# A fused transformer block on one core: V and the softmax weights on head-major partitions, all softmax results through DRAM, and a new order

## The chip, the cores and the metric

The kernel runs on one core of one Trainium2 chip. The metric is the device time of one execution in microseconds, as a median over runs: 238.28 us (three runs, 237.95 to 239.0). A core has five engines with queues of their own: TensorE (PE: matmuls, with weight loads as PEld), VectorE (DVE), ScalarE (ACT), GpSimd (POOL) and SyncE (SP), which here only issues transfers. Each engine executes its instructions strictly in the order in which the program gives them, and waits on semaphores for the others.

## The reference

The program is one block with adaptive layer norm, on x of 2048 positions and 512 features. A conditioning vector gives six modulation vectors. Attention has 32 heads of 16 features and looks back over eight positions, two apart.

```python
mod = (_silu(c) @ w_mod).reshape(c.shape[0], 6, 1, -1)       # sa, ca, ga, sb, cb, gb
h = _layernorm(x) * (1 + ca) + sa
q, k, v = split(h @ wqkv)                                    # 32 heads of 16
idx = pos[:, None] - arange(8) * 2                           # window of 8, step 2; negative ones masked
attn = softmax(where(mask, (q . k[idx]) * 16 ** -0.5, -1e9))
x = x + ga * (sum_w(attn * v[idx]) @ wo)
h = _layernorm(x) * (1 + cb) + sb
x = x + gb * ((gelu(h @ w_gate) * (h @ w_up)) @ w_down)      # hidden 1792
```

Inputs and outputs are bf16.

## The kernel before

The 2048 positions are worked in four groups (`sg` 0 to 3) of 512. For each group the steps are:

- **Norm and transposition.** DVE and ACT take the statistics of x (`bn_stats`, or sums on ACT), POOL raises to the power −0.5 (`rstd`), DVE normalises (`xn`). The result is transposed to features on partitions (`hT`), on PE for group 0 and 1, by a transposing transfer for 2 and 3.
- **Projections.** Twelve sets of four 128x512 matmuls give q, k and v (`qkv_ps`), which ACT copies to SBUF as bf16 (`qT`, `kT`, `vT`). Partition p of these holds features of head p // 4.
- **Logits.** For each of four feature slices j, DVE multiplies `qT` with eight shifted views of `kT` in one instruction of 128x4096 (`pq`). PE sums over the features of a head with narrow matmuls, 32 columns wide and four side by side, against the constant `Mph`: eight for each j (`LTp`).
- **Softmax.** DVE takes the maximum over the window, subtracts, ACT applies exp, DVE sums, inverts and multiplies (`e`): partitions are head and quarter of the positions.
- **Weights times V.** The weights are needed on other partitions (`PT`: four window places times 32 heads). For group 0 sixteen narrow PE transposes (`PTp`) and two ACT copies make `PT`; groups 1 to 3 store `e` to DRAM (`escr`) and read it back in four loads. V takes a similar way: `vT` is stored in one DRAM array `vscr` for all positions, and four loads, each to 32 partitions, put the four shifted copies into `V`, in runs of 1040 bytes. POOL zeroes the start of `V` for group 0. DVE multiplies `PT` and `V` for each j (`pv`, 128x4096), PE sums over the four places and two halves with `Msum` (`o_ps`), ACT copies (`oT`).
- **Output projection, second norm, FFN.** `x_ps`, then the norm again (`h`), 14 pairs of gate and up projections (`g_ps`, `u_ps`), GELU and copy on ACT, their product on DVE (`hht`), and the down projection (`y_ps`).

The order is not found by a scheduler at run time. Every step is a generator (a "thread") that yields operations with their engine; the table `ORDER` lists which thread is advanced next, so this one list of numbers sets the order of the instructions on each engine and of the transfers in SP's queue. A transfer that waits holds up everything issued behind it. The steps that the change touches are `setup` (POOL's constants), `qkv_ev` (copies of v), `vload`, `soft` and `pt_dma` (weights), `pv` and `pv_mm`. The head of the program also has 17 matmuls on zeros (`warm_ps`) which compute nothing that is used, and the products of the modulation vectors (`modT_ps`, `gR_ps`).

Of the kernel before, what the change touches and what calls it, by code (L numbers as in the profile page):

```python
# [16 lines left out]
PT_DMA = (1, 2, 3)  # L17

ORDER = [
# [87 lines left out]
def kernel(  # L107
# [13 lines left out]
    nc = tc.nc  # L121
# [4 lines left out]
    SG = 512  # L126
    NSG = S // SG
    CPS = SG // P
    DT = D // P
    FT = F // P  # L130
    VH = 16
    VR = S + VH

    def pool(name, bufs, **kw):
        return ctx.enter_context(tc.tile_pool(name=name, bufs=bufs, **kw))

    const = pool("const", 1)
    wts = pool("wts", 1)
# [554 lines left out]
    def soft(sg):  # L693
# [38 lines left out]

        if sg in PT_DMA:
            return
# [250 lines left out]
```

## Time and profile before

| | |
|---|---|
| median of three runs | 238.28 us (237.95 to 239.0) |
| the profiled execution, from first to last instruction | 235.7 us |
| PE busy | 229.0 us, 97% |
| DVE busy | 170.0 us, 72% |
| ACT busy | 150.5 us, 64% |
| POOL busy | 23.6 us, 10% |
| granted clock of PE | 1.00 in every stretch |
| moved by transfers | 30.21 MB, 128 GB/s in the mean |

The profile gives no time of its own for the execution apart from this span; the 2.6 us to the median lie outside the first and last instruction or between executions. A row of a timeline reads: start in us, length in us, engine, line of the kernel, operation, what is written and read, shape, count; in brackets the idle time of the engine before it and what ended it. A row can hold several instructions (x4); its length runs to the end of the last, and matmuls overlap, so the starts of neighbouring rows tell more than lengths. In the list of groups the numbers behind the bar are the busy time, the mean of one in ns, and the idle time in front with its releaser. In the list of transfers they are KB each and the median us from issue to landing.

### The profile page before, as it was taken

What the parts mean: (1) busy time and instruction counts of PE and PEld (TensorE: products, weight loads), DVE (VectorE), ACT (ScalarE), POOL (GpSimd) and SP (SyncE); (2) the same over time, 40 slices, a digit from 0 to 9 for tenths busy, and PEclk for the clock granted to TensorE, in tenths of its full rate; (3) what the DMA queues carried; (4) which work ended last, traced back from release to release, by engine and by line L of the source; (5) the groups of instructions that cost most, each with busy time, mean ns of one, the idle gap of its engine ahead of it and who ended that gap; (6) DMA issues with size and microseconds to landing.
All of it is one profiled execution on the core that took longest, in us unless ns stands there. A gap on an engine that the chain in (4) does not pass through costs nothing.

```text
span 235.7 us, 3655 instructions
## 1 busy us (share of the span) xinstructions
PE 229.0 (97%) x1376; PEld 108.6 (46%) x1388; DVE 170.0 (72%) x240; ACT 150.5 (64%) x283; POOL 23.6 (10%) x43
## 2 busy tenths in 40 slices
PE   7899899999999999999999999999999999999995
PEld 2755355434644444443444444444444444444443
DVE  3898999999999999989899787259295421222222
ACT  4799978796997558943867592446737325667400
POOL 2525471000100000040000010000001000000000
PEclk9999999999999999999999999999999999999999
DMA  6997987999969929607301972520000061000011
GB/s 212 375 361 210 209 214 138 217 376 347 195 161 241 298 75 201 112 3 178 90 0 32 211 123 48 144 56 0 0 3 1 22 134 45 3 0 0 0 47 45
DMA packets 36265, 30.21 MB, mean 128 GB/s; under 512 B 14872, under 2 KB 34328, under 8 KB 36248
## 3 DMA queue, kind: packets, MB, share of 16 engines
q1 hardware_dynamic: 35968, 29.72, 49.7%
q8 instruction: 11, 0.18, 0.4%
q10 hardware_dynamic: 280, 0.26, 0.3%
q14 instruction: 6, 0.05, 0.1%
HBM read 22.37 MB, written 4.98 MB: 116 GB/s over the span
## 4 chain that ended last, share of the span: by engine, by line
PE 79%; DVE 10%; DMA 5%; POOL 3%; issue 1%; ACT 0%; DVEq 0%; POOLq 0%
PE g_ps L851 21%; PE u_ps L851 21%; PE y_ps L863 14%; PE qkv_ps L606 11%; PE x_ps L818 6%; DMA x<-in_A_x_dram 5%; DVE pq L671 4%; PE o_ps L797 3%; POOL rstd L471 3%; PE LTp L685 2%; DVE xn L448 1%; PE y_ps L875 1%; DVE pv L778 1%; DVE st L430 1%; DVE e L729 1%
## 5 line engine op out<-in xcount | busy, mean ns | idle before, releaser
L851 PE MATMUL g_ps<-h,Wg 128*128 128x512 bf16 x224 | 57.5, 379 | 0.0
L851 PE MATMUL u_ps<-h,Wu 128*128 128x512 bf16 x224 | 57.5, 379 | 0.0
L863 PE MATMUL y_ps<-Wd,hht 128*128 128x512 bf16 x203 | 45.6, 379 | 0.4
L885 ACT ACTIVATE gl<-g_ps 128x512 bf16<-128x512 f32 x56 | 33.7, 601 | 17.5 <-PE g_ps L851 15.4
L892 ACT CAST ub<-u_ps 128x512 bf16<-128x512 f32 x56 | 32.9, 587 | 16.2 <-PE u_ps L851 16.1
L606 PE MATMUL qkv_ps<-hT,wqkv 128*128 128x512 bf16 x180 | 41.0, 380 | 0.0
L903 DVE TENSOR_TENSOR hht<-gl,ub 128x512 bf16<-128x512 bf16 x56 | 23.0, 421 | 24.4 <-ACT ub L892 24.4
L778 DVE TENSOR_TENSOR pv<-PT,V 128x4096 bf16<-128x4096 bf16 x16 | 36.0, 2288 | 3.0 <-DMA PT<-escr 3.0
L671 DVE TENSOR_TENSOR pq<-qT,kT 128x4096 bf16<-128x4096 bf16 x16 | 36.4, 2296 | 0.0
L851 PEld LDWEIGHTS <-Wg 128*128 128x128 bf16 x224 | 21.7, 98 | 26.9 <-issue 1.3
L851 PEld LDWEIGHTS <-Wu 128*128 128x128 bf16 x224 | 21.7, 98 | 26.8 <-issue 0.8
L863 PEld LDWEIGHTS <-hht 128*128 128x128 bf16 x210 | 20.6, 98 | 24.7
L606 PEld LDWEIGHTS <-wqkv 128*128 128x128 bf16 x180 | 19.6, 114 | 18.6 <-issue 2.3
L471 POOL TENSOR_TENSOR rstd<-rstd,neghalf 128x4 f32<-128x4 f32 (+1 forms) x9 | 12.8, 1427 | 149.0 <-DVE rstd L460 77.6
L910 DVE TENSOR_TENSOR ot<-y_ps,x 128x512 bf16<-128x512 f32 x15 | 10.2, 690 | 20.0 <-PE y_ps L863 19.8
L532 ACT ACTIVATE h<-h,modT,scl 128x512 bf16<-128x512 bf16 x12 | 8.8, 805 | 20.3 <-DMA h<-xn 20.3
L818 PE MATMUL x_ps<-woP,oT 128*128 128x512 bf16 x60 | 15.1, 379 | 0.2
L430 DVE BATCH_NORM_STATS2 st<-x 128x6 f32<-128x512 bf16 x19 | 12.9, 677 | 3.1 <-DMA x<-in_A_x_dram 2.9
L827 DVE TENSOR_TENSOR x<-x_ps,x 128x512 bf16<-128x512 f32 x16 | 10.8, 688 | 5.4 <-PE x_ps L818 5.3
L808 ACT CAST oT<-o_ps 128x512 bf16<-128x512 f32 x16 | 8.8, 588 | 4.3 <-PE o_ps L797 4.3
L408 ACT ACTIVATE gl<-x 128x512 bf16<-128x512 bf16 x13 | 8.3, 645 | 3.2 <-DVE x L827 2.9
L685 PE MATMUL LTp<-pq,Mph 128*32 128x512 bf16 x128 | 9.1, 382 | 1.3 <-DVE pq L671 1.3
(85 smaller groups left out, 184.7 us busy)
## 6 DMA issues: line engine op xcount, KB each, us to landing
V<-vscr SPq DMA_DIRECT2D x12, 520.0 KB, 10.5
wm<-in_w_mod_dram SPq DMA_DIRECT2D x6, 512.0 KB, 5.3
vscr<-vT SPq DMA_DIRECT2D x4, 512.0 KB, 4.3
out_dram<-ot SPq DMA_DIRECT2D x15, 128.0 KB, 1.7
Wg<-in_B_w_gate_dram SPq DMA_DIRECT2D x1, 1792.0 KB, 9.8
Wu<-in_B_w_up_dram SPq DMA_DIRECT2D x1, 1792.0 KB
wqkv<-in_A_wqkv_dram SPq DMA_DIRECT2D x3, 512.0 KB, 8.8
x<-in_A_x_dram SPq DMA_DIRECT2D x3, 512.0 KB, 9.2
```

Source lines behind the costliest of these rows:

```text
L430: nc.vector.bn_stats(out=st[:], in_=src()[:, c4, :])
L471: nc.gpsimd.tensor_tensor(out=k["rstd"][:, a:b], in0=k["rstd"][:, a:b], in1=neghalf[:, a:b], op=ALU.pow)
L606: nc.tensor.matmul(ps[:], lhsT=wqkv[blk][:, dt, j::4], rhs=B["hT", sg][:, :, dt, :], start=(dt == 0), stop=(dt == DT - 1))
L671: nc.vector.tensor_tensor(out=pq[:], in0=_ap(B["qT", sg][:, j, :], [[0, W], [1, SG]]), in1=_ap(kT[:, j, sg % 3 * SG + 2:sg % 3 * SG + 2 + ...
L685: nc.tensor.matmul(B["LT", sg][H * g:H * g + H, 4 * t:4 * t + 4, :], lhsT=M[:], rhs=B["pq", sg, j][:, 4 * t:4 * t + 4, g * P:(g + 1) * P], ...
L778: nc.vector.tensor_tensor(out=t[:], in0=_ap(B["PT", sg][:, 0, :], [[SG, 2], [0, 4], [1, SG]]), in1=_ap(v[:, 0, j, :], [[8, 2], [4 * (SG + ...
L818: nc.tensor.matmul(ps[:], lhsT=B["oT", sg][:, j, c4::CPS] if sg else B["oT", sg][:, j, c4 * P:(c4 + 1) * P], rhs=woP[:, j, :], start=(j == ...
L851: nc.tensor.matmul(ps[:], lhsT=Wt[:, dt, ft * P:(ft + 1) * P], rhs=B["h2T", sg][:, :, dt, :], start=(dt == 0), stop=(dt == DT - 1))
L863: nc.tensor.matmul(ps[:], lhsT=B["hh", sg, ft][:, c4 * P:(c4 + 1) * P], rhs=B["Wd", ft // 4][:, ft % 4, :], start=(ft == 0), stop=(ft == F ...
L885: nc.scalar.activation(out=gl[:], in_=B["g", sg, ft][:], func=ACT.Gelu_apprx_tanh)
L892: nc.scalar.copy(out=ub[:], in_=B["u", sg, ft][:])
L903: nc.vector.tensor_tensor(out=hh[:], in0=B["gl", sg, ft][:], in1=B["ub", sg, ft][:], op=ALU.mult)
```

## The change

Four things change together.

**V.** The copy of v goes to one lasting tile `vT` with 16 columns of halo in front: POOL zeroes them for group 0, and for each later group a small ACT copy moves the last 16 columns to the front (`vh`), after the store of the group before has been read. Each group has a DRAM array of its own, stored in one piece with its halo. The four loads of a group now take one feature slice each, for all 128 partitions: a partition is head and window place (4h + a), a run is 4208 bytes, and the product with slice i waits for load i alone.

**Weights.** `e` is written with the window places in the order that makes the loads plain (the same instruction with a rearranged output), stored for all four groups, and read back in two loads of 128 partitions. Group 0's PE transposes and ACT copies are gone. Since partitions are head-major now, the sum over places uses the logits' constant `Mph`; `Msum` and POOL's set-up of it and of V's zeros are gone. `wo` is loaded with its rows in the order that fits.

**Buffers.** `ssum` uses the tile of `mx`; the pool of `vT` is gone.

**Order.** `ORDER` is new as a whole (847 operations where there were 850).

```diff
-PT_DMA = (1, 2, 3)
 ORDER = [
-    23, 23, 23, 23, 23, 23, 23, 2, 33, 1, 23, 1, 0, 23, 0, 22, 31, 23, 23, 31, 31, 2, 33, 22, 23, 23, 22, 23,
+    23, 23, 23, 23, 23, 23, 0, 0, 23, 23, 23, 23, 23, 23, 23, 23, 23, 23, 23, 2, 1, 33, 33, 33, 33, 33, 1, 22,
...
-    vscr = dram.tile([P, 4, VR], BF16, name="vscr")
+    vscr = [dram.tile([P, 4, VL], BF16, name=f"vscr{g}") for g in range(NSG)]
-    escr = {g: dram.tile([P, W, P], BF16, name=f"escr{g}") for g in PT_DMA}
+    escr = {g: dram.tile([P, 4, 2, P], BF16, name=f"escr{g}") for g in range(NSG)}
+    vT = const.tile([P, 4, VL], BF16, name="vT")
...
-            nc.gpsimd.memset(M2[:], 0.0)
-            for w4 in range(4):
-                nc.gpsimd.affine_select(out=M2[:], in_=M2[:], pattern=[[-1, H]], compare_op=ALU.not_equal, fill=1.0,
-                                        base=-H * w4, channel_multiplier=1)
-            B["V4", 0] = T("v4", [P, 4, 4, SG + 8], BF16, "V4")
-            for w4 in range(4):
-                nc.gpsimd.memset(B["V4", 0][H * w4:H * w4 + H, :, :, 0:8 + 2 * w4].rearrange("p i j s -> p (i j) s"), 0.0)
-        yield Op("POOL", 3.0, f2, take=[SL["v4"]], fire="M2", after=["LN1.0.rs2"])
+            nc.gpsimd.memset(vT[:, :, 0:VH], 0.0)
+        yield Op("POOL", 0.2, f2, fire="kz", after=["LN1.0.rs2"])
...
+            if sg and (blk, j) == (2, 0):
+                yield Op("ACT", 0.25, lambda: nc.scalar.copy(out=vT[:, :, 0:VH], in_=vT[:, :, SG:VL]), after=[f"vst.{sg - 1}"], fire=f"vh.{sg}")
...
-        for w4 in range(4):
-            def f(w4=w4):
-                src = bass.AP(vscr.tensor, vscr.offset + VH + sg * SG - 8 - 2 * w4 + z,
-                              [[16 * VR, H], [VR, 16], [1, SG + 8 - z]])
-                    out=B["V4", sg][H * w4:H * w4 + H, :, :, z:SG + 8].rearrange("p i j s -> p (i j) s"), in_=src)
+        for i in range(4):
+            def f(i=i):
+                n = 4 * VL - 8
+                src = bass.AP(vscr[sg].tensor, vscr[sg].offset + i * 4 * VL + 2, [[16 * VL, H], [2, 4], [1, n]])
+                nc.sync.dma_start(out=B["V4", sg][:, i, :, :].rearrange("p j s -> p (j s)")[:, 0:n], in_=src)
...
-                        nc.tensor.matmul(PTp[H * (3 - a):H * (3 - a) + H, :, q:q + P], lhsT=ident[:, H * g:H * g + H],
-                                         rhs=B["e", sg][:, a::4, :], start=True, stop=True,
-            yield Op("ACT", 0.49, f, after=[f"ptp.{sg}"], give=[SL["att"]], fire=f"pt.{sg}.{h}")
...
-        for a in range(4):
-                src = bass.AP(escr[sg].tensor, escr[sg].offset + a * P,
-                              [[W * P, H], [4 * P, 2], [H * W * P, CPS], [1, P]])
+        for t in range(2):
+                src = bass.AP(escr[sg].tensor, escr[sg].offset + t * P, [[2 * P, P], [H * W * P, CPS], [1, P]])
+                nc.sync.dma_start(out=B["PT", sg][:, t, :].rearrange("p (g s) -> p g s", s=P), in_=src)
...
-                                        in1=_ap(v[:, 0, j, :], [[8, 2], [4 * (SG + 8), 4], [1, SG]]), op=ALU.mult)
-            yield Op("DVE", 2.2, f, after=[f"pt.{sg}.1", f"V4ld.{sg}"], take=[SL["prod"]] * heads(GV[sg]).get(j, 0),
+                                        in1=_ap(v[:, j, 0, :], [[8, 2], [VL, 4], [1, SG]]), op=ALU.mult)
+            yield Op("DVE", 2.2, f, after=[f"pt.{sg}.1", f"V4.{sg}.{j}"], take=[SL["prod"]] * heads(GV[sg]).get(j, 0),
...
-                            nc.tensor.matmul(o_ps[H * i:H * i + H, :], lhsT=M2[:], rhs=B["pv", sg, j][:, t, i, :],
+                            nc.tensor.matmul(o_ps[H * i:H * i + H, :], lhsT=M[:], rhs=B["pv", sg, j][:, t, i, :],
```

What the new table does is seen at three places. Line numbers differ between the two programs, since the second is shorter.

SP's queue from its first transfer, before (`x` is a block of 512 positions, its first half of group 0 comes by ACT's queue; `wm` are modulation weights, `wqkv_128` the query weights):

```order
L231 DMA x<-in_A_x_dram 128x2x512
L245 DMA wm_204<-in_w_mod_dram 128x4x512 x2
L223 DMA wqkv_128<-in_A_wqkv_dram 128x4x512
L231 DMA x<-in_A_x_dram 128x2048
L223 DMA wqkv_129<-in_A_wqkv_dram 128x4x512
```

and in the change, where `wqkv_129` names the query weights:

```order
L224 DMA x<-in_A_x_dram 128x2x512
L224 DMA x<-in_A_x_dram 128x2048
L238 DMA wm_239<-in_w_mod_dram 128x4x512 x2
L216 DMA wqkv_129<-in_A_wqkv_dram 128x4x512
L224 DMA x<-in_A_x_dram 128x2048
```

The x block of group 1 moved from behind the query weights to ahead of the modulation weights.

DVE from the last statistics before the first product to the weights of group 0, before:

```order
L448 TENSOR_SCALAR xn<-x,sums,rstd 128x512
L671 TENSOR_TENSOR pq<-qT,kT 128x4096
L448 TENSOR_SCALAR xn<-x,mv,rstd 128x512 x3
L671 TENSOR_TENSOR pq<-qT,kT 128x4096 x4
L697 TENSOR_TENSOR LTp<-LTp,maskT 32x8x16
L702 TENSOR_REDUCE mx<-LTp 128x128
L708 TENSOR_TENSOR LTp<-LTp,mx 128x1024
L718 TENSOR_REDUCE ssum<-LTp 128x128
L724 RECIPROCAL rinv<-ssum 128x128
L729 TENSOR_TENSOR e<-LTp,rinv 128x1024
```

and in the change:

```order
L441 TENSOR_SCALAR xn<-x,mv,rstd 128x512
L661 TENSOR_TENSOR pq<-qT,kT 128x4096 x4
L441 TENSOR_SCALAR xn<-x,mv,rstd 128x512 x2
L441 TENSOR_SCALAR xn<-x,sums,rstd 128x512
L687 TENSOR_TENSOR LTp<-LTp,maskT 32x8x16
L692 TENSOR_REDUCE mx<-LTp 128x128
L698 TENSOR_TENSOR LTp<-LTp,mx 128x1024
L661 TENSOR_TENSOR pq<-qT,kT 128x4096
L708 TENSOR_REDUCE mx<-LTp 128x128
L714 RECIPROCAL rinv<-mx 128x128
L719 TENSOR_TENSOR e<-LTp,rinv 128x2x4x128
```

The four products of group 0 now stand in a run, with the rest of group 2's normalisation behind them instead of behind the first. In both, one product of group 1 stands between the subtraction and the sum.

SP's queue around the weights and V of group 0 in the change (before, it has no `escr` or `PT` there, and the four loads of V in slices of 32 partitions):

```order
L635 DMA vscr_102<-vT 128x2112
L216 DMA woP<-in_A_wo_dram 32x4x512
L231 DMA wm<-in_w_mod_dram 128x4x512
L483 DMA_TRANSPOSE hT<-xn 128x16x128
L643 DMA V_569<-vscr_102 128x1x2104 x2
L635 DMA vscr_103<-vT 128x2112
L726 DMA escr_108<-e 128x1024
L643 DMA V_569<-vscr_102 128x1x2104
L312 DMA gscr_106<-gR 4x128
L734 DMA PT<-escr_108 128x4x128 x2
```

A store of the weights of group 0 and two loads of them are new there; one quarter of V stands between the store and the loads, and the store of V of group 1 ahead of them.

More of the change, by code (lines that the diff above doesn't have):

```diff
@@ L131 @@
     VH = 16
-    VR = S + VH
+    VL = SG + VH
     def pool(name, bufs, **kw):
@@ L155 @@
     M = const.tile([P, H], BF16, name="Mph")
-    M2 = const.tile([P, H], BF16, name="Msum")
     maskT = const.tile([H, W, 16], F32, name="maskT")
@@ L672, in f @@
                                         in1=_ap(kT[:, j, sg % 3 * SG + 2:sg % 3 * SG + 2 + SG], [[2, W], [1, SG]]), op=ALU.mult)
-            yield Op("DVE", 2.2, f, after=[f"qkv.{sg}.1.{j}", f"qkv.{sg}.0.{j}", f"qkv.{sg - 1}.1.{j}" if sg else "M2"] + ["halo"] * (sg == 3), take=[SL["prod"]] * heads(GL[sg]).get(j, 0),
+            yield Op("DVE", 2.2, f, after=[f"qkv.{sg}.1.{j}", f"qkv.{sg}.0.{j}", f"qkv.{sg - 1}.1.{j}" if sg else "kz"] + ["halo"] * (sg == 3), take=[SL["prod"]] * heads(GL[sg]).get(j, 0),
                      give=[SL["q"]] if j == 3 else [], fire=f"pq.{sg}.{j}")
@@ L758, in pt_dma, with f @@
         yield Op("SP", 0.65, f, after=[f"p.{sg}"], give=[SL["es"]], fire=f"est.{sg}", lat=0.4)
-        for a in range(4):
-            def f(a=a):
-                if a == 0:
+        for t in range(2):
+            def f(t=t):
+                if t == 0:
                     B["PT", sg] = smp["PT"].tile([P, 2, SG], BF16, name="PT")
-                src = bass.AP(escr[sg].tensor, escr[sg].offset + a * P,
-                              [[W * P, H], [4 * P, 2], [H * W * P, CPS], [1, P]])
-                nc.sync.dma_start(out=B["PT", sg][H * (3 - a):H * (3 - a) + H, :, :].rearrange("p t (g s) -> p t g s", s=P),
-                                  in_=src)
-            yield Op("SP", 0.65, f, after=[f"est.{sg}", f"pv.{sg - 1}.3"], take=[SL["PT"]] if a == 0 else [],
-                     fire=f"ptl.{sg}.{a}" if a < 3 else f"pt.{sg}.1", lat=0.6)
-    smp = {k: pool(k + "_p", 1) for k in ("mx", "e", "ssum", "rinv", "PT")}
+                src = bass.AP(escr[sg].tensor, escr[sg].offset + t * P, [[2 * P, P], [H * W * P, CPS], [1, P]])
+                nc.sync.dma_start(out=B["PT", sg][:, t, :].rearrange("p (g s) -> p g s", s=P), in_=src)
+            yield Op("SP", 0.65, f, after=[f"est.{sg}"] + ([f"pv.{sg - 1}.3"] if sg else []), take=[SL["PT"]] if t == 0 else [],
+                     fire=f"pt.{sg}.{t}", lat=0.6)
+    smp = {k: pool(k + "_p", 1) for k in ("mx", "e", "rinv", "PT")}
     def pv(sg):
```

51 lines of the change are left out of this document (16 added, 35 removed), and 68 rows, old and new, of the table ORDER.

## The prediction

> **What bounds the kernel now.** I read the page's totals and slices first, then busy time by stretch, then PE's timeline row by row.
>
> ```profile
> span 235.7 us, 3655 instructions
> PE 229.0 (97%) x1376; PEld 108.6 (46%) x1388; DVE 170.0 (72%) x240; ACT 150.5 (64%) x283; POOL 23.6 (10%) x43
> 11.00:67.00 56.00, 54.99 (x405) 28.24 (x405) 54.52 (x68) 49.44 (x108) 13.34 (x8) 1.00 0.94 247
> 130.00:236.00 106.00, 102.55 (x507) 47.62 (x512) 48.71 (x90) 51.27 (x83) 2.05 (x2) 1.00 0.22 48
> ```
>
> The last two rows are stretches: start:end, length, then busy time of PE, PEld, DVE, ACT, POOL, the granted clock, the DMA share and GB/s. From 11 to 67 us PE and DVE are both full (55.0 and 54.5 of 56 us); after 130 us PE alone is. Since busy PE overlaps itself, I check it against the starts of its runs:
>
> ```profile
> 9.81 2.78 PE L579 MATMUL qkv_ps<-hT,wqkv 128*128 128x256 bf16 x24
> 21.08 1.03 PE L606 MATMUL qkv_ps<-hT,wqkv 128*128 128x512 bf16 x4
> 22.04 0.61 PE L685 MATMUL LTp<-pq,Mph 128*32 128x512 bf16 x8
> 22.59 4.51 PE L606 MATMUL qkv_ps<-hT,wqkv 128*128 128x512 bf16 x20
> 27.03 1.05 PE L685 MATMUL LTp<-pq,Mph 128*32 128x512 bf16 x16
> 28.82 0.61 PE L685 MATMUL LTp<-pq,Mph 128*32 128x512 bf16 x8 [0.74 <-DVE pq L671]
> 29.37 10.55 PE L606 MATMUL qkv_ps<-hT,wqkv 128*128 128x512 bf16 x48
> 39.85 0.62 PE L743 MATMUL PTp<-e,ident 128*32 128x256 bf16 x16
> 40.40 4.50 PE L606 MATMUL qkv_ps<-hT,wqkv 128*128 128x512 bf16 x20
> 50.92 0.61 PE L797 MATMUL o_ps<-pv,Msum 128*32 128x512 bf16 x8
> 51.75 0.62 PE L797 MATMUL o_ps<-pv,Msum 128*32 128x512 bf16 x8 [0.21 <-DVE pv L778]
> 110.50 1.05 PE L685 MATMUL LTp<-pq,Mph 128*32 128x512 bf16 x16
> 112.08 0.62 PE L685 MATMUL LTp<-pq,Mph 128*32 128x512 bf16 x8 [0.53 <-DVE pq L671]
> 229.70 3.22 PE L875 MATMUL y_ps<-Wd,hht 128*128 128x384 bf16 x28
> ```
>
> 48 matmuls take 39.85 − 29.37 = 10.48 us: 0.216 us each plus a change of shape. Four take 0.86, so between 21.08 and 22.04 about 0.10 goes to changing to the narrow shape; from 22.04 to 22.59 eight narrow ones take 0.43 and the change back 0.12. By this ruler PE waits visibly in three places: 27.03 + 0.87 to 28.82 is 0.92 us, 50.92 + 0.47 to 51.75 is 0.36, 110.50 + 0.87 to 112.08 is 0.71: **2.0 us, each time for a DVE product**. From the first query matmul (9.81) on, PE's instructions at these prices add up to some 220.5 us (my count by line); its last row ends at 229.70 + 3.22 = 232.92. So 0.6 us more of waits is spread thinly, and 2.8 us of tail stays. The change can gain only in the head, in PE's own work, and in the waits. V's transfers hold up no row of PE.
>
> **Head.** The new order puts the second x block (512 KB) in SP's queue ahead of the two modulation blocks and the query weights.
>
> ```profile
> 8.07 0.55 PE L348 MATMUL modT_ps<-scT,wm 128*128 128x1 bf16 x16 [0.58 <-DMA wm<-in_w_mod_dram]
> 10.84 0.63 ACT L408 ACTIVATE gl<-x 128x512 bf16<-128x512 bf16 x1 [0.23 <-DMA x<-in_A_x_dram]
> ```
>
> PE waits until 8.07 for the second modulation block; the query weights and that x block come next, the latter at 10.84. Two blocks in 2.77 us are 1.39 each. One block more ahead delays the modulation to 9.46; the 1.74 us from there to the first query matmul (9.81 − 8.07) stay, since the same writes of hT follow. Start: 11.2, **+1.4** (1.0 if the queue overlaps better, 1.5 from 0.1 of DVE work put between).
>
> **PE's own work.** The 16 PTp transposes go (0.65 with both changes of shape), and by my count of PE's order ten blocks of narrow matmuls stand where thirteen stood; two of the missing three are joined to others, 0.22 each. The rest is the same instructions: **−1.1** (−0.9 to −1.2). The two ACT copies of PT and POOL's set-up of the summing matrix and of V's zeros go as well; three small ACT copies of V's halo come. I price them at nothing: ACT is busy 49.44 of 56 us in the early stretch and POOL 13.34, and the products need POOL's zeros only at 17 us, when the old, longer set-up would also be done. Were that cover gone, ACT's part would be under 1 us either way.
>
> **First logits.** The new DVE order does all four products of group 0 in a run; the old one put a normalisation of group 2 behind the first and waited for POOL there.
>
> ```profile
> 9.02 1.77 DVE L547 TENSOR_SCALAR hT<-hTp,mod 128x256 bf16<-128x256 bf16 x5 [0.19 <-PE hTp L514]
> 13.37 0.17 DVE L460 TENSOR_SCALAR rstd<-mv 128x3 f32<-128x3 f32 x1
> 17.59 2.29 DVE L671 TENSOR_TENSOR pq<-qT,kT 128x4096 bf16<-128x4096 bf16 x1
> 20.78 1.06 DVE L448 TENSOR_SCALAR xn<-x,mv,rstd 128x512 bf16<-128x512 bf16 x3 [0.90 <-POOL rstd L471]
> 22.07 8.90 DVE L671 TENSOR_TENSOR pq<-qT,kT 128x4096 bf16<-128x4096 bf16 x4
> 30.88 0.28 DVE L697 TENSOR_TENSOR LTp<-LTp,maskT 32x128 f32<-32x128 f32 x1
> 38.17 1.23 DVE L729 TENSOR_TENSOR e<-LTp,rinv 128x1024 bf16<-128x1024 f32 x1
> 39.31 1.38 DVE L448 TENSOR_SCALAR xn<-x,sums,rstd 128x512 bf16<-128x512 bf16 x4
> ```
>
> New: the five hT writes end near 12.5 (the head's 1.4 and one more xn ahead). Three statistics with their aggregates follow (10.84 to 13.37: 2.5), four small ones (0.5), five xn (1.7): the first product starts near 17.2 (17.0 to 17.8) and the fourth ends 8.9 later, at 26.1. PE needs 22.04 − 9.81 = 12.2 us from its start to the first logits set, then three sets (1.3), one projection (0.86) and changes: it asks for the fourth product at about 25.8. Wait **0.3** (0 to 1.0) in place of 0.92.
>
> **Weights of group 0 through DRAM.** This path becomes longer: before, e ends at 39.40 and PT is in SBUF two ACT copies later, 41.5. Now e is stored and two loads wait for the landing.
>
> ```profile
> 40.44 1.08 ACT L752 CAST PT<-PTp 128x512 bf16<-128x512 f32 x2
> 109.86 0.33 SPq L757 DMA_DIRECT2D escr<-e  x1
> 111.96 2.95 SPq L765 DMA_DIRECT2D PT<-escr  x4
> 146.89 0.86 SPq L757 DMA_DIRECT2D escr<-e  x1
> 150.10 3.75 SPq L765 DMA_DIRECT2D PT<-escr  x4
> PT<-escr SPq DMA_DIRECT2D x12, 64.0 KB, 2.4
> V<-vscr SPq DMA_DIRECT2D x12, 520.0 KB, 10.5
> 78.93 6.69 DVE L778 TENSOR_TENSOR pv<-PT,V 128x4096 bf16<-128x4096 bf16 x3
> 85.68 0.61 PE L797 MATMUL o_ps<-pv,Msum 128*32 128x512 bf16 x8
> ```
>
> The first PT load is issued 2.1 to 3.2 us after the store; with two issues instead of four (0.7 to 0.9 each) the last follows under 1 us later and lands in 2.4: 5.2 to 6.6 us, up to 1.5 more because a quarter of V (about 540 KB) is issued in between. New e ends at 26.1 + 1.0 (three xn) + 8.4 (the stretch 30.88 to 39.40, less 0.1) = 35.5, so PT is there at 41.8 (40.7 to 43.6). DVE, after two more products and the four xn, asks at 41.3: it waits 0.5 (0 to 2.3), and everything queued behind that product on DVE moves too. PE feels it where it stands closest behind DVE, at group 1's last output set: before, the product ends at 85.6 and PE starts at 85.68, no margin. New, DVE is 1.2 earlier there (0.4 by its start, 0.9 by the POOL wait, less 0.1) and PE about 0.4 earlier (+1.4 − 0.9 of its work − 0.92 − 0.36 + 0.3): margin 0.8. Loss on PE **0** (0 to 1.5).
>
> **Second group's last logits.** At 112.08 PE waited for a product behind which DVE had put a normalisation waiting for POOL. Now the rescaling subtraction covers POOL's 1 us, and two of the three products are done by about 108, PE asking at 110.5: the 0.71 goes, as does the 0.36 at 51.75.
>
> **V.**
>
> ```profile
> L778 DVE TENSOR_TENSOR pv<-PT,V 128x4096 bf16<-128x4096 bf16 x16 | 36.0, 2288 | 3.0 <-DMA PT<-escr 3.0
> ```
>
> Before, the products with V waited 3.0 us in all, and for PT, not V. A dense quarter over all partitions instead of a slice over 32 should land sooner than the 10.5 us quoted; the product that needs it has other DVE work ahead. Worth nothing, unless the quarters hold up PT (above).
>
> **Sum.** 232.92 + 1.4 − 1.1 − 2.0 + 0.3 + 0 + 0.4 = 231.9. The last 0.4 is an allowance for waits that a wholly new order brings and that I do not see; the old order's unassigned 0.6 is its size (0 to 1). PE ends 1.0 earlier, the span is 234.7. The profiled 235.7 stands 2.6 below the median 238.28; I carry the difference over: **237.3**.
>
> **Rivals.**
> *More is gained* (236.0): neither the 0.4 nor the 0.3 nor the old 0.6 is paid. For it: DVE's first 40 us lose the 0.90 wait; against: 54.52 of 56 us leave no slack to catch a slip.
> *PT late, slower* (240.2): store and loads queue behind V's store and quarter, so that PT lands 9.5 us after e, at 45.0. DVE waits 3.7, PE loses 3.7 − 0.8 = 2.9. It makes the kernel slower by 0.5% from a wait of 3.0 on, that is 8.8 us after e; the third store-and-load above, 6.96 to its last issue's end, comes nearest, but with four issues.
> *PE's clock falls back in the head, slower* (239.5).
>
> ```profile
> 1.24 4.45 PE L217 MATMUL warm_ps<-gB 128*128 128x512 bf16 x10 [1.24 <-DVE gB L212]
> 5.74 1.38 PE L217 MATMUL warm_ps<-gB 128*128 128x512 bf16 x5
> ```
>
> The first ten filler matmuls take 4.4 us, about 0.43 each, the next five 0.22 each: PE starts at half speed. The old order kept fillers for the gaps up to 9.6 us; the new one spends nearly all by 7 us and leaves PE mostly idle until 11.2. If it falls back for as long as the first ten lasted, half of that, 2.2 us, is lost, and the products shift with it. Against: some twenty transposes and modulation sets stand in the gap. [...]
> *V's new reading brings the gain* (faster V, as such): then DVE would stall on V before, and the group's row names PT alone. Little chance (no result apart from the forecast's), kept inside it.
>
> **Numbers.** This kernel's measurement can tell 0.5% (1.2 us) from no change. The forecast and cases near it: 0.45, within 0.5%. More gained: 0.35, faster. PT late 0.10 and cold clock 0.10, slower. Range: below, the rival's 236.0 and a little of the floor under it; above, the cold clock and half of a late PT: 235.9 to 239.8. The forecast's own range is 236.2 to 238.7.
>
> **What would show it.** First query matmul at 11.2; the first product at 17.2; the wait before the fourth logits set under 1 us; PT landing within 6.5 us of e; no wait near 112; last PE row ending near 231.9. Wrong if PE's matmuls after 11 us run at 0.43, or if PE waits for products of group 0 or 1 by over 1.5 us.

## The result and the profile after

The changed kernel took 236.22 us (median of four, 236.18 to 236.97) where the kernel before took 238.12: ratio 0.9923, 95% interval 0.99 to 0.9947. In a later job twelve more executions gave 237.21 (236.41 to 238.51) against 238.0: ratio 0.9969 (0.9952 to 0.9986). The change is faster by 0.3 to 0.8%, and about half of the difference between the two medians has a reason that the experiments found.

First the profile of the changed kernel beside the rows that the prediction showed of before. PE's timeline (start, duration, engine, line, operation, count, wait in brackets):

```profile
span 234.5 us, 3613 instructions
...
1.24 6.38 PE L210 MATMUL warm_ps<-gB 128*128 128x512 bf16 x16 [1.24 <-DVE gB L205]
...
11.09 2.78 PE L572 MATMUL qkv_ps<-hT,wqkv 128*128 128x256 bf16 x24
...
25.75 0.62 PE L675 MATMUL LTp<-pq,Mph 128*32 128x512 bf16 x8 [0.22 <-DVE pq L661]
...
85.07 0.62 PE L765 MATMUL o_ps<-pv,Mph 128*32 128x512 bf16 x8 [0.16 <-DVE pv L746]
...
109.89 1.48 PE L675 MATMUL LTp<-pq,Mph 128*32 128x512 bf16 x24
...
228.39 3.22 PE L843 MATMUL y_ps<-Wd,hht 128*128 128x384 bf16 x28
```

The first query matmul starts at 11.09, the fourth logits set waits about 0.3, the wait near 112 is gone (24 matmuls in a row at 109.89), and PE ends at 231.61, 1.31 before the old 232.92. The wait at 85.07 is new: the eight narrow matmuls ahead of it start at 84.30 and end at 84.73 by the ruler of 0.43 a set, so PE waits 0.34 for a product. DVE's and SP's timelines:

```profile
16.80 8.89 DVE L661 TENSOR_TENSOR pq<-qT,kT 128x4096 bf16<-128x4096 bf16 x4
...
33.74 1.22 DVE L719 TENSOR_TENSOR e<-LTp,rinv 128x1024 bf16<-128x1024 f32 x1
34.88 2.28 DVE L661 TENSOR_TENSOR pq<-qT,kT 128x4096 bf16<-128x4096 bf16 x1
37.08 0.16 DVE L458 TENSOR_SCALAR rstd<-sums 128x4 f32<-128x4 f32 x1
38.37 1.38 DVE L441 TENSOR_SCALAR xn<-x,sums,rstd 128x512 bf16<-128x512 bf16 x4 [1.13 <-POOL rstd L464]
39.67 2.29 DVE L661 TENSOR_TENSOR pq<-qT,kT 128x4096 bf16<-128x4096 bf16 x1
41.87 8.89 DVE L746 TENSOR_TENSOR pv<-PT,V 128x4096 bf16<-128x4096 bf16 x4
...
76.12 8.89 DVE L746 TENSOR_TENSOR pv<-PT,V 128x4096 bf16<-128x4096 bf16 x4
```

```profile
34.99 0.33 SPq L726 DMA_DIRECT2D escr<-e  x1
35.37 0.52 SPq L643 DMA_DIRECT2D V<-vscr  x1
...
37.27 0.92 SPq L734 DMA_DIRECT2D PT<-escr  x2
```

PT's loads are issued 2.3 us after the store, and DVE does not wait for it at 41.87. It lost 1.13 us to POOL shortly before, at 38.37. The two sums of DVE's busy time that carry the reading of all runs, from DVE's first statistics to the end of the last product of group 1 with V (85.6 before, 85.0 after), of before and of after:

```profile
4.10:85.60 81.50, 79.31 (x100) 1.00 0.92 251
```

```profile
4.10:85.00 80.90, 78.82 (x100) 1.00 0.78 251
```

**DVE is busy for 97% of the time from 4.1 to 85 us in both kernels.** By the same view PE is busy for 98% of it and more (79.9 of 81.5 us before, 79.8 of 80.9 after), so the shares alone do not tell which of the two sets the time. The wait at 85.07 and the runs below say that it is DVE, and that PE follows it. Of the 1.2 us of span, 0.6 is gained up to that product and 0.6 behind it. A third piece lies outside the span: the profiled execution's own time is 236.26, 1.76 above it. In the old kernel's executions the time lies 2.15 to 2.37 above the span; in the changed one's 1.67 to 1.89 in twelve of sixteen, and up to 3.07 in the rest.

### The profile page after: what moved, and what is told of

It reads as the page before. It is cut to its first block, busy times and chain, and to the rows that moved or that the text cites. A ratio compares the mean times of both kernels' runs of the same rounds, so it can differ in the third digit from the quotient of the medians.

```text
span 234.5 us, 3613 instructions
## 1 busy us (share of the span) xinstructions
PE 228.6 (97%) x1361; PEld 109.2 (47%) x1372; DVE 169.2 (72%) x240; ACT 148.8 (63%) x284; POOL 13.8 (6%) x35
## 4 chain that ended last, share of the span: by engine, by line
PE 62%; DVE 15%; issue 2%; POOL 0%; DVEq 0%; POOLq 0%
PE y_ps L831 19%; PE g_ps L819 17%; PE u_ps L819 17%; DVE pv L746 5%; DVE pq L661 5%; PE x_ps L786 4%; PE o_ps L765 2%; PE y_ps L843 1%; DVE x L795 1%; PE LTp L675 1%; DVE hht L871 1%; DVE st L423 1%; DVE xn L441 1%; DVE e L719 1%; DVE woP L384 1%
## 5 line engine op out<-in xcount | busy, mean ns | idle before, releaser
L871 DVE TENSOR_TENSOR hht<-gl,ub 128x512 bf16<-128x512 bf16 x56 | 22.5, 419 | 30.3 <-ACT ub L860 30.1
L599 PE MATMUL qkv_ps<-hT,wqkv 128*128 128x512 bf16 x180 | 40.3, 380 | 0.0
L464 POOL TENSOR_TENSOR rstd<-rstd,neghalf 128x4 f32<-128x4 f32 (+1 forms) x9 | 8.8, 980 | 132.8 <-DVE rstd L458 69.9
L795 DVE TENSOR_TENSOR x<-x_ps,x 128x512 bf16<-128x512 f32 x16 | 10.5, 680 | 1.2 <-PE x_ps L786 1.2
L621 ACT CAST kT<-qkv_ps 128x512 bf16<-128x512 f32 x16 | 9.5, 597 | 2.3 <-PE qkv_ps L599 2.2
L786 PEld LDWEIGHTS <-oT 128*128 128x128 bf16 x64 | 6.9, 110 | 7.1 <-issue 0.4
```

What stands on the lines that cost most here:

```text
L599: nc.tensor.matmul(ps[:], lhsT=wqkv[blk][:, dt, j::4], rhs=B["hT", sg][:, :, dt, :], start=(dt == 0), stop=(dt == DT - 1))
L786: nc.tensor.matmul(ps[:], lhsT=B["oT", sg][:, j, c4::CPS] if sg else B["oT", sg][:, j, c4 * P:(c4 + 1) * P], rhs=woP[:, j, :], start=(j == ...
L795: nc.vector.tensor_tensor(out=x[:, c4, :], in0=B["x1ps", sg, c4][:], in1=x[:, c4, :], op=ALU.add)
L871: nc.vector.tensor_tensor(out=hh[:], in0=B["gl", sg, ft][:], in1=B["ub", sg, ft][:], op=ALU.mult)
```

## The experiments

All were run in five rounds beside the kernel before (238.0 in each job). Ratios are to it, with 95% intervals; spans are of the profiled execution.

| run | edit | us | ratio | span |
|---|---|---|---|---|
| b_products_run | before, first four products in a run | 242.74 | 1.0214 (1.0194 to 1.0234) | 240.4 |
| b_rstd_early | before, one root earlier | 238.12 | 1.0011 (1.0002 to 1.0019) | 235.9 |
| b_x1_early | before, with the new head | 240.22 | 1.0097 (1.0082 to 1.0111) | 237.2 |
| b_logits3_early | before, one product earlier | 239.58 | 1.0068 (1.0056 to 1.008) | 237.0 |
| new_code_old_order | changed code, old order | 241.67 | 1.016 (1.0135 to 1.0184) | 239.0 |
| old_code_new_order | old code, changed order | 244.82 | 1.0287 (1.0268 to 1.0306) | 243.1 |
| a_x1_late | changed, head undone | 238.03 | 0.9997 (0.9983 to 1.0012) | 236.6 |
| a_v_order_only | changed, V's loads together | 239.31 | 1.0064 (1.0035 to 1.0093) | 238.0 |
| a_v_slices | same, four slices of 32 partitions | 238.72 | 1.0041 (1.0018 to 1.0064) | 238.3 |
| a_pt_late | changed, one more copy before PT | 238.90 | 1.0035 (1.0006 to 1.0063) | 237.6 |
| after_again | changed | 237.21 | 0.9969 (0.9952 to 0.9986) | 236.3 |
| a_fillers | changed, five fillers more | 236.42 | 0.9932 (0.992 to 0.9944) | 234.6 |

In edits of the order, names are those of its operations: `pq.0.1` is the second product of group 0, `LN1.2.x0` the first normalisation of group 2, `LN2.1.va0` the small statistics step ahead of POOL's root. Each row tells what stands on the engine, before (−) and now (+).

### Order and code apart

New code in the old order, and old code in the new order:

```diff
 SP, old order:
-(p.0) ptp.0 on PE, pt.0.0 and pt.0.1 on ACT
+(p.0) est.0  pt.0.0  pt.0.1
```

> The changed code (V and the weights on head-major partitions, dense quarters, all weights through DRAM) in the order of before: the sixteen transposes and two copies drop out of it, the store and two loads of group 0's weights stand right behind e, the three small halo copies ahead of each group's V copies. Theory (the code by itself brings no gain; the new order lets it do so): PT of group 0 lands about 5.5 us after e, which ends at 39.4, so near 45; DVE asked at 42.8 and waits 2 us, PE loses 2 at the second group's last output set, where it has no margin, and gains 0.65 of its own work, partly hidden in that: 239.3 (238.5 to 240). Rival (V's new reading and the transposes that go are the gain): 237.0.

The code alone costs 3.7 us. Timeline of DVE and of PE:

```profile
38.24 1.22 DVE L719 TENSOR_TENSOR e<-LTp,rinv 128x1024 bf16<-128x1024 f32 x1
...
44.81 8.89 DVE L746 TENSOR_TENSOR pv<-PT,V 128x4096 bf16<-128x4096 bf16 x4 [1.85 <-DMA PT<-escr]
```

```profile
114.69 0.72 PE L819 MATMUL g_ps<-h,Wg 128*128 128x512 bf16 x2
115.74 0.38 PE L819 MATMUL g_ps<-h,Wg 128*128 128x512 bf16 x1 [0.33 <-ACT h L525]
...
116.66 1.02 PE L819 MATMUL u_ps<-h,Wu 128*128 128x512 bf16 x4
```

PT lands 5.3 us after e, as expected, and DVE waits 1.85. The rest was not foreseen: PE then also waits for the second norm at 115 (the four g matmuls take 1.97 from their start to that of u, where the kernel before has 0.88), and the median lies 2.4 above the forecast. The profiled execution is the fastest of the five, 240.72; what makes the others longer is not shown. The sixteen transposes that are gone brought no gain that the time shows.

```diff
 SP, new order with old code:
-V4.0.0 V4.0.1 ... est.0 V4.0.2 ... V4.0.3
+V4.0.0 V4.0.1 V4.0.2 V4ld.0 ... (the same for groups 1 to 3)
```

> The code of before in the changed order: group 0's weights through sixteen transposes on PE, which stand right behind e; V in four slices over 32 partitions each, all four where the changed order has a group's first quarter; POOL's set-up of the summing matrix early, behind the first two reciprocal roots. Theory (the order is the gain): everything as in the changed kernel plus the 0.65 us of the transposes: 236.9 (236.5 to 237.4) against 236.2 of the changed kernel and 238.1 of before. Rival (V's new reading is the gain, or the order only works with it): 238 or more.

A miss by 8 us, on the rival's side. Rows of DVE and ACT:

```profile
43.40 4.49 DVE L779 TENSOR_TENSOR pv<-PT,V 128x4096 bf16<-128x4096 bf16 x2 [1.31 <-DMA V<-vscr]
```

```profile
44.92 2.05 ACT L633 CAST vT<-qkv_ps 128x512 bf16<-128x512 f32 x4 [5.35 <-DMA vscr<-vT]
```

The old slices land 9.1 us after issue (in the groups of DMA issues: `V<-vscr`, 12 loads of 520 KB, median 9.1) and the store of group 1's V, issued behind the four of group 0, is late: ACT waits 5.35 for it. The stores of V land as follows, in this run and in the changed kernel:

```profile
vscr<-vT SPq DMA_DIRECT2D x4, 512.0 KB, 12.1
```

```profile
vscr<-vT SPq DMA_DIRECT2D x4, 528.0 KB, 3.9
```

So neither half is a gain here: each is slower than before by itself, and only together are they faster. An additive sum over parts could not have shown that. Two things come along with the order in this run and are not separated from it. All four loads of V stand where the changed order has the first quarter, which costs the changed code 2.1 us as well (next section), and behind the waits, at 45.55, 20 projection matmuls take 7.07 us where 20 take 4.51 in the kernel before (22.59); the granted clock of the profiled execution is 0.986 in the mean, that of the other three 0.993.

### V's reading

```diff
 a_v_order_only (SP): V4.0.2 V4.0.3 ahead of est.0; V4.1.1-3 directly behind V4.1.0; V4.3.3 behind V4.3.2
 a_v_slices, besides:
-src = bass.AP(..., i * 4 * VL + 2, [[16 * VL, H], [2, 4], [1, 4 * VL - 8]])   # quarter i, 128 partitions
+src = bass.AP(..., 2 + 2 * i, [[16 * VL, H], [VL, 16], [1, VL - 8]])          # partitions i::4
-after=[f"pt.{sg}.1", f"V4.{sg}.{j}"]
+after=[f"pt.{sg}.1", f"V4.{sg}.3"]
```

> The changed kernel, with the four loads of V issued together for groups 0, 1 and 3 (the third and fourth of group 0 ahead of the store of e, and so on); quarters as they are. It is the control for the next kernel. Theory: quarters land within 6 us of their issue, V is there long before the products, the store of group 1's V is delayed by little: 236.2 to 236.8. Rival (loads issued together hold up the store of e or group 1's V): 237.5 or more.

> The same order as the control, but each of the four loads of V brings one of the four window offsets for all of V, into 32 partitions (every fourth one) in rows of 1040 bytes, so that every product waits for all four loads. Old code in the new order lost 6.8 us, with slices over 32 neighbouring partitions that landed 9 us after issue, a wait of 1.31 us for V and 5.35 us of ACT behind the store of group 1's V. Theory 1 (a transfer over 32 partitions is slow, wherever they are): slices land after 9 us or more, the same two waits come, 241 or more. Theory 2 (32 neighbouring partitions are what is slow): slices land in about 6 us, no wait for V, within 0.6 of the control. Rival (the prediction: V's reading is worth nothing, and what was lost there was another thing): within 0.6 of the control, with slices at 9 us.

The control is slower than the changed kernel by 2.1 us (1.8 between the executions at full clock, 0.998 and more, with medians of 238.5 and 236.7). SP's and DVE's timelines say why:

```profile
36.31 0.33 SPq L726 DMA_DIRECT2D escr<-e  x1
...
42.09 0.92 SPq L734 DMA_DIRECT2D PT<-escr  x2
```

```profile
45.31 8.90 DVE L746 TENSOR_TENSOR pv<-PT,V 128x4096 bf16<-128x4096 bf16 x4 [2.03 <-DMA PT<-escr]
```

With all of group 0's V issued by 33, the store of e needs 5.8 us until PT may be issued, not 2.3, and PT is there 9.0 after e. This is the prediction's second rival, by the transfers that it named. In issues and landing times of the two kernels the slices are as fast as the quarters:

```profile
V<-vscr SPq DMA_DIRECT2D x16, 526.0 KB, 7.6
```

```profile
V<-vscr SPq DMA_DIRECT2D x16, 520.0 KB, 7.5
```

The times of the two agree too: at full clock the medians are 238.5 and 238.6. Slices over 32 neighbouring partitions have higher medians, 9.1 us in the old code in the new order and 10.5 in the kernel before. So it isn't 32 partitions that are slow but, by these numbers, 32 neighbouring ones. Transfers of the other groups run beside these loads, and no run exchanges one kind for the other with all else equal; the cause is not shown. What quarters alone allow is to spread the loads: each product needs one of them, so two can be issued behind the store of e.

### How late PT may be

```diff
 nc.sync.dma_start(out=escr[0][:], in_=e)
+nc.sync.dma_start(out=hop[:], in_=escr[0][:])
-src = escr[0] ...
+src = hop ...
```

> The changed kernel, in which group 0's weights go through one more copy from DRAM to DRAM between the store and the two loads. The copy costs about 2.3 us until the next transfer may start, as the store did (34.99 to 37.27). Theory: the weights land at 43 to 44 in place of 40.5 to 42, DVE waits 1 to 2.3 us where it waited 0, and as DVE is full until the last output set of group 1, where PE already waits 0.34 us, PE loses all of it: 237.2 to 238.5. Rival (the prediction's margin of 0.8 on PE): 0.8 less, 236.4 to 237.7; rival (the weights have more time than that, nothing waits): 236.2.

```profile
44.91 8.90 DVE L751 TENSOR_TENSOR pv<-PT,V 128x4096 bf16<-128x4096 bf16 x4 [1.52 <-DMA PT<-hop]
...
79.16 8.89 DVE L751 TENSOR_TENSOR pv<-PT,V 128x4096 bf16<-128x4096 bf16 x4
```

The wait is 1.52, and the median is 1.7 above that of the changed kernel in twelve executions, where 1.0 to 2.3 was expected; the level, 238.90, is 0.4 above the forecast, because five of the twelve executions have a fallen clock (0.992 to 0.993; below); the other seven have a median of 237.9. In the profiles, the last product of group 1 ends 1.3 later than in the later profile of the changed kernel (86.77), whose head ran alike but 0.24 later, and the span is 1.3 longer. PE has no margin of 0.8; it loses all.

### The head

```diff
 SP:  x0.0 [-x1] wm1 wm0 wqkv0 [+x1 +wqkv1] x2 ...
 DVE: LN1.1.st0-2 from between LN1.0's steps to behind LN1.0.h2.1;  ACT: LN1.1 sums and squares behind LN1.0.h3.1
```

> The changed kernel with its head undone: the second x block is loaded behind the first query weights (and the key weights behind it), and group 1's three statistics and the sums on ACT stand behind the writes of hT. Theory: PE's first query matmul comes at 9.9 in place of 11.1, but the three statistics (2.4 us), which the changed order puts into DVE's wait for the modulation blocks, now stand ahead of the first product, which starts at 17.6 in place of 16.8; PE waits at the fourth logits set for what it gained and 0.8 more, DVE is full until 85, and the kernel is slower by 0.8 to 1.5: 237.0 to 237.7 (the upper end where group 2's transposed rows, which POOL finishes 1.3 us ahead of PE, come late). Rival (the prediction's sum, in which the later start is a cost of 1.3 by itself): 235.0.

PE's first query matmul is 0.8 earlier, at 10.29, and the gain is gone. DVE's timeline:

```profile
9.43 0.17 DVE L348 TENSOR_TENSOR mod<-modT_ps,c 128x8 f32<-128x8 f32 x1 [0.98 <-PE modT_ps L341]
...
18.53 8.89 DVE L661 TENSOR_TENSOR pq<-qT,kT 128x4096 bf16<-128x4096 bf16 x4
...
78.17 8.89 DVE L746 TENSOR_TENSOR pv<-PT,V 128x4096 bf16<-128x4096 bf16 x4
```

The first product starts 1.73 later, the last of group 1 ends 2.05 later, the span is 2.1 longer in these two profiles. Between the medians at full clock it is 1.3 (238.0 and 236.7), as expected, at a level 0.3 above the forecast. DVE now stands idle for 0.98 while PE works off fillers ahead of the modulation sets; the statistics used to fill that time. The later start of PE in the changed kernel is thus no cost: what PE gains ahead of DVE it waits for (1.25 for ACT's copies at 15.18, 0.60 for the fourth product at 27.48).

The converse, the new head in the old order:

```diff
 SP:  x0.0 [+x1] wm1 wm0 wqkv0 [-x1] wqkv1 ...
 DVE: LN1.0.st2 [+LN1.1.st0] ... LN1.0.x1 [+LN1.1.st1 st2] LN1.0.x2 ...
```

> The kernel before with the head of the changed one alone: the second x block is loaded ahead of the modulation blocks, and the three statistics of group 1 with ACT's sums fill DVE's and ACT's waits there. Theory (DVE sets the pace up to the second group's last output set: from its first statistics at 4.1 to the end of that product at 85.6 it is idle for 2.17 us in all, and the span ends 150.1 after it): a later start of PE costs nothing, DVE can gain its two waits of the head (0.27 and 0.19) at most, and the 0.90 for POOL's root stays: 237.6 to 238.0, or 1.4 more in executions in which the clock falls back. Rival (the prediction's sum, in which PE's start, 1.3 later, is a cost): 239.4.

```profile
18.73 0.15 DVE L466 TENSOR_SCALAR rstd<-sums 128x1 f32<-128x1 f32 x1 [1.85 <-ACT gl L420]
```

Slower by 2.2, past the prediction's rival, and past the 1.4 that the theory allowed for the clock. All four executions had a granted clock of 0.993. In the profiled one the matmuls of the head are long: eight transposes take 1.01 us at 9.37 (0.61 at 20.85), the filler at 11.45 takes 0.63 (0.38 in the kernel before), and the 24 query matmuls 3.09, 0.3 more than in the changed kernel. The query matmuls start at 11.88, 0.8 later than there, although DVE begins its writes of hT only 0.16 later. In this order ACT copies the queries ahead of group 2's squares, so whatever makes PE late reaches DVE by way of ACT: 1.85 there. The run does not separate PE's later start from the fallen clock. That a later start costs nothing is shown for the changed order only.

### Waits for POOL, and the last logits

```diff
 DVE: pq.0.0 [-LN1.2.x0 x1 x2 x3] pq.0.1 pq.0.2 pq.0.3 [+LN1.2.x0 x1 x2 x3] pq.1.0
```

> The kernel before, with one edit: the four normalisations of group 2 (and the transposing DMA behind them) stand behind the four products of group 0 and no longer behind the first. Theory (the order of the first logits is a part of the gain): DVE's 0.90 us wait for POOL goes, the fourth product ends near 26.5 instead of 28.7, the wait of 0.92 on PE ahead of the fourth logits set goes, and the last PE row ends 0.9 earlier: about 237.2 against 238.1. POOL's reciprocal root at 17.43 took 3.31 us beside a product and 1.0 elsewhere; here nobody waits for it. Rival (DVE is full to 67 us, so what is gained at 28 us is lost by 52): within 0.3 of before.

Slower by 4.7. POOL's and PE's timelines:

```profile
17.39 9.91 POOL L472 TENSOR_TENSOR rstd<-rstd,neghalf 128x4 f32<-128x4 f32 x1 [2.62 <-DVE rstd L466]
```

```profile
36.45 0.38 PE L607 MATMUL qkv_ps<-hT,wqkv 128*128 128x512 bf16 x1 [1.80 <-POOL hT L531]
```

The root stands for 9.91 us, until 0.86 after the last of four products, and DVE's wait of 0.90 for it is still there, behind them. Group 2's rows come late, and PE waits for them (1.80, then three times 0.37). The changed order has the run of four too, but its root starts at 15.19, 1.6 ahead of the first product, and takes 1.25.

```diff
 DVE: [+LN2.1.va0] z.2 [-LN2.1.va0] pq.3.1 LN2.1.x0 ...
```

> The kernel before, with one edit: the small statistics instruction of group 1's second normalisation, and POOL's reciprocal root that follows it, stand ahead of the rescaling of group 2 and no longer behind it. Theory: POOL's instruction falls beside the rescaling and not beside a product, so it takes 1.0 us in place of 2.92; DVE's wait of 0.90 goes, the product that PE waited for at 112.08 ends 0.9 earlier, PE's wait of 0.71 goes: 237.4 against 238.1. Rival (POOL's instruction is as long as it is for another reason than the product beside it): POOL stays near 2.9, no change. Second rival: the 0.71 is lost again behind 112, no change with POOL at 1.0.

```profile
100.66 0.17 DVE L466 TENSOR_SCALAR rstd<-sums 128x4 f32<-128x4 f32 x1 [0.99 <-ACT gl L420]
```

POOL's part came true (1.01 in place of 2.92), the gain didn't: the step now waits 0.99 for ACT's squares.

```diff
 DVE: ot.0.0 ot.0.1 [+pq.3.2] s1.2 ri.2 p.2 [-pq.3.2] ot.0.2
```

> The kernel before with one edit: the third product of the last group's logits stands ahead of group 2's sum, reciprocal and scaling, no longer behind them. With the root early (the run on that) nothing was gained, as the statistics then waited 0.99 us for ACT's squares and the product ended no sooner. Theory (behind 85 us PE alone sets the time, so a wait taken away there is gained): the product ends near 109, PE's 0.71 at 112 goes, e of that group comes 2.2 later, with 7 us to spare before PE needs its output: 237.3 against 238.0. Rival (the weights of that group now come late for DVE and PE, which eats the gain): 238.0.

```profile
111.98 1.48 PE L686 MATMUL LTp<-pq,Mph 128*32 128x512 bf16 x24 [1.51 <-DVE e L730]
```

Slower by 1.6, though the product was early. PE waits for e of the group before: the logits have a single PSUM buffer (`"lg": 1`), which e frees. So it takes both for the 0.71 us at 112: e early, and two products done by the time PE asks. DVE there, before and in the changed kernel:

```profile
108.61 1.22 DVE L729 TENSOR_TENSOR e<-LTp,rinv 128x1024 bf16<-128x1024 f32 x1
```

```profile
104.44 1.23 DVE L719 TENSOR_TENSOR e<-LTp,rinv 128x1024 bf16<-128x1024 f32 x1
...
106.17 4.49 DVE L661 TENSOR_TENSOR pq<-qT,kT 128x4096 bf16<-128x4096 bf16 x2
```

In the changed order e ends at 105.66, 4.2 earlier than before, with two products behind it; by these rows and the two runs that is how the 0.6 behind 85 us came. No run moves e alone.

### The clock in the head

> The changed kernel, unchanged, in more executions. In three of the kernels that share its head, 13 of the 24 query matmuls took 0.213 us each in place of 0.109 (11.27 to 13.98), and the first product came 1.0 to 1.2 later: there the clock fell back in the head, the rival that the prediction priced at 2.2 and 0.10. Theory (whether it falls is a matter of each execution, since the head is the same): a part of the executions here lies at 236.2 and a part 1.4 higher, near 237.6, so that the median comes to between 236.2 and 237.6. Rival (it belongs to those three kernels): all executions within 0.4 of 236.2.

Four of the twelve executions have a granted clock of 0.993 and spans of 235.8 to 236.4; in the others it is 1.0, with spans of 234.6 to 235.6. In the profiled one the query matmuls took 4.48 us in place of 2.78. Its PE by stretches (busy, count, granted clock, DMA share, GB/s):

```profile
8.00:11.40 3.40, 2.55 (x50) 0.99 1.07 373
11.40:14.80 3.40, 3.40 (x18) 0.50 1.10 368
```

**The clock fell to half for 3.4 us**, behind a stretch in which PE had, but for the first query matmuls, only transposes and one-column matmuls. The query matmuls lose 1.7, and the first product comes 1.3 later; the price reaches DVE by way of ACT, whose squares stand behind the query copies:

```profile
16.03 0.15 DVE L458 TENSOR_SCALAR rstd<-sums 128x1 f32<-128x1 f32 x1 [0.86 <-ACT gl L412]
...
18.11 6.70 DVE L661 TENSOR_TENSOR pq<-qT,kT 128x4096 bf16<-128x4096 bf16 x3
...
77.88 8.89 DVE L746 TENSOR_TENSOR pv<-PT,V 128x4096 bf16<-128x4096 bf16 x4
```

The execution shown with the result ran the same instructions in this stretch and kept its clock. What differs ahead of it is when PE came to full speed, which I read from the length of the fillers (0.43 us each at first, 0.22 later; the column of the granted clock reads 1.00 for both). The sixteen took 6.38 us there and less here:

```profile
1.23 5.25 PE L210 MATMUL warm_ps<-gB 128*128 128x512 bf16 x16 [1.23 <-DVE gB L205]
```

At 0.21 saved by each, that is about five fillers fewer at half speed, so PE came to full speed some 2.3 us earlier (an estimate), and stood idle sooner. Without the four executions the median is 236.7, which is still 0.5 above that of the first four; what makes this rest stays open.

```diff
 PE: scp w16 [+w17] th0 mp1 th1 mp0 [+w18 +w19] th2 [+w20] th3 [+w21] qph.0
-pl.spawn(warmup(13, 17))
+pl.spawn(warmup(13, 22))
```

> The changed kernel with five more filler matmuls in PE's waits of the head: one ahead of the first transposes, two behind the second modulation set, one each behind the third and fourth transposes, just ahead of the query matmuls (where the order before had one). Theory (PE's clock falls back for want of work between 7.9 and 11.1): the 24 query matmuls take 2.78 us in all executions, which lie within 0.4 of each other, at 236.2 to 236.5. Rival (five fillers are too few, or the clock falls for another reason): two heights as in the changed kernel. Rival (the fillers stand in the way of the third transposes): 0.4 to 0.6 later in all.

```profile
8.00:11.40 3.40, 2.92 (x52) 1.00 1.07 370
11.40:14.80 3.40, 3.40 (x29) 1.00 1.10 366
```

All five executions lie between 236.2 and 236.5 with a clock of 1.0, where the changed kernel has 237.21 in the same job. In the profiled one PE came to full speed early as well (the first sixteen fillers took 5.13 us), and the clock did not fall. **This is the changed kernel without its slow third, as far as five executions tell**: with falls in 4 of 16, as in the changed kernel, five in a row would come out clean with a chance of 0.24 even without the new fillers (an estimate, 0.75 to the fifth power).

## Why the prediction was right, and where not

The forecast was 237.3 (235.9 to 239.8); 236.22 and 237.21 were measured. The span came to 234.5 where 234.7 was forecast. The terms:

- **Start, first product, fourth set, PT, 112.** 11.09 for 11.2; 16.80 for 17.2, 0.2 under its range; a wait of 0.3 for 0.3; no wait for PT where 0.5 (0 to 2.3) was allowed; no wait at 112; PE's end at 231.61 for 231.9. These steps hold.
- **"Start +1.4" and "PE's own work −1.1" as terms of the end.** The sizes were about right, the account was wrong. PE started 1.28 later and ended 1.31 sooner; with the old 2.0 of waits gone and the new 0.3 and 0.34 added, −1.24 remains for its own work. Up to 85 us the time is DVE's. In the seven profiles of the changed order with the changed code, the span ends 149.5 us after group 1's last product with V:

| | product ends | span | difference |
|---|---|---|---|
| changed | 85.01 | 234.5 | 149.5 |
| a_fillers | 85.09 | 234.6 | 149.5 |
| after_again | 86.77 | 236.3 | 149.5 |
| a_x1_late | 87.06 | 236.6 | 149.5 |
| a_pt_late | 88.05 | 237.6 | 149.6 |
| a_v_order_only | 88.45 | 238.0 | 149.6 |
| a_v_slices | 88.81 | 238.3 | 149.5 |

  Before, it was 85.62 and 150.1, and three more kernels in the old order have 150.1 to 150.2 with that product ending between 85.7 and 90.3 (b_rstd_early, b_x1_early, b_products_run). Three runs in which PE also waits behind the product have more: old_code_new_order 151.2, new_code_old_order 151.3, b_logits3_early 151.5. So 0.6 was gained on DVE and 0.6 behind it, and a sum of PE's starts and waits met the total because PE ends up where DVE lets it. That it met the span within 0.2 is luck in part: the 1.13 below was in no term, and the allowance of 0.4 for unseen waits happened to be the size of the wait at 85.07. On DVE the 0.90 at 20.78 went, and the 0.27 and 0.19 in the head; 1.13 at 38.37 came, which I had not seen: the statistics step there stands directly ahead of the normalisation that needs POOL's root. These waits come to 0.2 of the 0.6. Most of the rest is DVE's own busy time, 79.31 before and 78.82 after for 100 instructions each; it is spread over many rows, and its cause stays open.
- **"Margin on PE at group 1's last output set 0.8, loss 0."** It failed: PE waits 0.34 there, so the margin was never there. DVE's product came 0.6 earlier and not 1.2, because of the 1.13 at 38.37, and PE asked for it 0.9 earlier and not 0.4. No loss came of it only because PT was in time. The price of the rival PT late, the wait less 0.8, should have been the whole wait, as the run with one more copy shows.
- **"V: worth nothing."** Right for the transfer as such (slices spread over all partitions equal quarters), wrong for the change. With V's loads together, PT comes 2.03 us late for DVE; the old slices in the new order lost more. Quarters let the loads be spread.
- **112.** The cause was told too simply: it took e 4.2 us earlier, through two products moved behind it, and not just the wait for POOL.
- **PE's clock falls back.** It was given 0.10 and 2.2 us. The profiled execution shown with the result has none of it, but 4 of 12 later ones do, at about 1.3 of span. The price was mis-sized because 2.2 assumed a fall as long as the first ten fillers, 4.4 us; it lasts 3.4 (after_again), which takes 1.7 from the query matmuls. The chance was mis-sized because I took the kernel to have one head, where the outcome differs from execution to execution. That a thinly filled stretch makes the clock fall was my assumption: no row of the profile before shows a fall. In the profiles the clock was 0.50 behind a stretch with 2.55 us of PE's work in 3.40 (after_again), and stayed at 1.00 behind 2.63 (changed) and 2.92 (a_fillers). When PE comes to full speed does not decide it by itself: with sixteen fillers in 5.25 us the clock fell and in 6.38 it held, but with 6.49 and 6.50 (a_v_order_only, a_v_slices) the query matmuls took 4.08 and 3.90 us. What decides it is not shown.
- **The rest outside the span**, 2.6, was carried over. It was 1.76, which is most of the difference between 237.3 and 236.22. The 2.6 was too large to begin with, as the median of three executions less the span of one; with time and span of the same execution the old kernel has 2.15 to 2.37. New code in the old order has 1.71 to 1.75 in four of its five executions (2.97 in the fifth), old code in the new order 2.2 to 2.33: it belongs to the code. What it consists of, the profile doesn't show, and it stays open.

## What to carry to other kernels

Where two engines are both busy for over 95% of a stretch, find the one instruction at which the other waits last, and sum on the engine that feeds it; here everything up to 85 us is read from one row of DVE. A rewrite and the order made for it are one thing: each half alone was slower by 1.6 to 2.9%, so pieces of an order are not worth what they save in isolation. When a new order thins out PE's work ahead of its first large matmuls, look at the granted clock of several executions, and try fillers in the waits rather than ahead of them; five executions of one kernel speak for that here.

## What the runs showed of the hardware

POOL's timeline before, and after:

```profile
17.43 3.31 POOL L471 TENSOR_TENSOR rstd<-rstd,neghalf 128x4 f32<-128x4 f32 x1 [2.65 <-DVE rstd L465]
26.89 6.99 POOL L530 TENSOR_SCALAR hT<-hT,mod 128x512 bf16<-128x512 bf16 x4 [6.15 <-DMA hT<-xn]
...
100.92 2.92 POOL L471 TENSOR_TENSOR rstd<-rstd,neghalf 128x4 f32<-128x4 f32 x1 [39.39 <-DVE rstd L465]
```

```profile
31.34 3.13 POOL L523 TENSOR_SCALAR hT<-hT,mod 128x512 bf16<-128x512 bf16 x4 [14.78 <-DMA hT<-xn]
37.33 1.01 POOL L464 TENSOR_TENSOR rstd<-rstd,neghalf 128x4 f32<-128x4 f32 x1 [2.86 <-DVE rstd L458]
```

POOL's root on 128x4 numbers takes 1.01 us alone, 2.92 and 3.31 beside one of DVE's products, and 9.91 beside four in a row (b_products_run): it ends 0.86 after the last, and does not get in between them. Moved from beside a product to beside the rescaling, it took 1.01 in place of 2.92 (b_rstd_early). POOL's four scalings of group 2's rows took 6.99 before, where products ran beside them, and 3.13 after. So in these rows an instruction of POOL is longer beside a product, and the run of four acts as one block. At 17.43, and at 17.39 in b_products_run, the root starts 0.16 us ahead of the product by the profile and is still the one that takes longer. The profile's times of POOL are rough, and what makes POOL wait is not shown.

With four quarters of V queued ahead of a store of 256 KB in place of two, the issue that waits for the store comes 5.8 us after it (36.31 to 42.09, a_v_order_only) and not 2.3 (34.99 to 37.27, changed kernel), though the store's own issue takes 0.33.
